# Sink attention in front of two expert layers: sink columns copied once, a row of steps one step later, a small scaling on another engine

## The chip, the cores and the metric

The kernel runs on one core of a Trainium2 chip. The time is that of one execution on the device, in microseconds (us). The core has five engines, each with a queue of its own that is worked off in order: TensorE (PE; PEld is its weight load), VectorE (DVE), ScalarE (ACT), GpSimd (POOL) and SyncE (SP), which only starts transfers here.

## The reference, cut to what matters

Three stages follow one another. The change touches only the first, and of it only batch 0 (and one preparation of the sink values in both batches).

```python
B, H, S, D = 2, 8, 768, 64; n_sink, window = 4, 128
scores = (q @ k.T) / sqrt(D)
keep = (key < n_sink) | ((query - key >= 0) & (query - key < window))
a = softmax(where(keep, scores, -1e9))
x = a @ v                                  # heads side by side: B, 768, 512
h = relu(x @ w_in)                         # 512 -> 1024; w_in, conv_w, w_out are float64
c = 3-tap convolution of h along the sequence, by conv_w
y = (h * sigmoid(c)) @ w_out               # 1024 -> 512
out = sum over 2 of 4 experts: w_e * causal_attention_e(y) @ wo_e
```

## The kernel before, in words

The sequence of 768 is cut into 6 tiles of 128 queries, and the 8 heads into 4 pairs. A step of the attention is one query tile `qt` and one head pair `pr`, so a batch has 24 steps, four to a tile. What belongs to one step is cut into stages (`S` scores, `T` transposes, `V` value products, `gather` and so on), and each stage has a lag in steps: at step t, the stage with lag L works on step t - L. `LAGS` holds the lags, and `ORD1` the order in which the stages of one step are written out; `run_phases` merges the stages of both batches and of the next layer by step and then by that order. So every engine's queue is a list fixed by hand. A stage with a third entry n works on n steps together, at the lag counted from the first of them. Batch 0's steps are followed by batch 1's, and from the sixth step of batch 1 on by those of the first expert layer.

In batch 0 the tiles `qt` 2 to 5 take an "overlaid" form (`a1_S_overlaid`, `a1_T_overlaid`), because with a window of 128 a query tile sees of the older key tile exactly the keys that it doesn't see of its own. Scores with the own key tile and with the older one go into two PSUM tiles (L515); VectorE overwrites one with the other where a mask says so (L518), takes the negative maximum of each row (L519) and scales it by 0.125 (L520); ScalarE takes the exponential with that as bias (L522), 132 columns wide for each head: 128 keys and 4 sink columns. The four sink columns come with the key tiles: an even key tile carries sinks 0 and 1 in front, an odd one must carry sinks 2 and 3 at its end. GpSimd copies them there (L511, 8 columns), once for each query tile 2 to 5, ahead of that tile's first scores.

The pairs `pr` 0 and 1, and 2 and 3, are transposed together (four transposes on TensorE, L571), copied from PSUM on ScalarE (L532), and split by GpSimd into the part of the own key tile and that of the older one (two selections, L575 and L577). The value products (L641) read these. The sink columns of the probabilities take another way: GpSimd gathers them pair by pair into a small tile `G` (L614) and, with the last pair, repeats that four times (L616); TensorE transposes it (`a1_sinkT`, L621), ScalarE copies it (L623), VectorE makes the low part of it (`a1_sinkL`, L628), and four products with the sink values `vsr` add it to the outputs (`a1_sinkV`, L649). The sums of the rows become reciprocals (`a1_r`), are transposed (`a1_rT`, L545), go to DRAM and come back spread over the partitions (L549, L556); `x_norm` multiplies the output by them (L560), `x_hi` and `x_lo` split the result into two parts (L532, L671), and `x_halo` copies edge columns.

`vsr` holds the sink values' high part in two groups of 32 partitions and the low part in the two others: ScalarE copies all (L295), then GpSimd subtracts in place in partitions 32 to 63 and 96 to 127, one instruction each (L299). Both sit in `tails`, a list from which each step takes one entry, in line with the pieces of a background job: the weights of the first expert layer, which arrive as float64, are decoded and split on VectorE and ScalarE during the attention (L343 to L353, L417, L538, L540).

The query, key and value tiles of the later part, the sums that come back and the outputs of most stages live in one pool of 18 SBUF buffers (tag `W`); a transfer into such a buffer waits for the last reader of what was there. PSUM has 8 banks under one tag (`B`), for scores, transposes and outputs alike.

Of the kernel before, what the change touches and what calls it, by code (L numbers as in the profile page):

```python
# [8 lines left out]
F32 = mybir.dt.float32  # L9
# [6 lines left out]
ALU = mybir.AluOpType  # L16
# [3 lines left out]
B, H, S, D = 2, 8, 768, 64  # L20
P = 128
NT = S // P
# [14 lines left out]
SCALE = 0.125  # L37
# [33 lines left out]
BG0 = 550  # L71
BG1 = 650
BG2 = 1200
LAGS = ((1, 2, 1, 5, 3, 4, 5, 5, 2, 7, 7, 9, 11), (1, 1, 2, 6, 3, 4, 5, 3, 2, 5, 6, 7, 7))
LAGM = (1, 2, 3)
A2_N = 2
EVT = 'aaadadada'
ORD1 = 'm.rest a0.more a1.T a0.gather m.more m.H a1.gather a1.rB m.gate a0.xl m.Y a1.S a1.V a1.sV a1.xl a1.r a0.S a1.halo a0.sL late a0.V a0.rB a0.sV a0.xm a1.more a1.sT a0.halo a0.rT a1.xm a1.misc a1.xh a0.sT a0.T a0.misc a1.sL a0.r a1.rT m.conv m.misc a0.xh'
ORD2 = 'q1 c0.V c0.T c0.S0 c1.V c1.T c1.S0 out c0.W c0.S1 qlo c0.norm c1.W in c1.S1 q0'
ENG_G = 'pp'  # L80
WHI = 'aadaddapdpaaddda'
# [7 lines left out]
class Kernel:  # L89
# [57 lines left out]
    def consts(self, pool):  # L147
        nc = self.nc
        self.words = pool.tile([P, 4], I32, name="words")
        self.ident = pool.tile([P, P], F32, name="ident")  # L150
        self.causal = pool.tile([P, 4 * P + 2], F32, name="causal")
        self.cw = pool.tile([P, 3 * NF], F32, name="cw")
        self.flag = pool.tile([P, 1], I32, name="flag")
        self.lims = pool.tile([P, 2], F32, name="lims")
        self.guard = pool.tile([P, 2 * NF + 1], F32, name="guard")
        self.ones = pool.tile([P, 1], F32, name="ones")
        self.nsink, self.window = self.lims[:, 0:1], self.lims[:, 1:2]
        self.m0 = pool.tile([P, P], F32, name="m0")
        self.m1 = pool.tile([P, 2 * P], F32, name="m1")
        self.mEO = [pool.tile([P, 2, KW], F32, name=f"m{i}x") for i in range(2)]  # L160
# [128 lines left out]

    def prep_vs(self, b, t):  # L290
        nc, vs = self.nc, t["vs"]

        def hi():
            t["vsr"] = self.pSm.tile([P, DM], F32R, tag="vsr", bufs=1, name=self.nm("vsr"))
            nc.scalar.copy(t["vsr"], vs)  # L295

        def lo(g):
            sl = slice(g, g + 32)
            nc.gpsimd.tensor_tensor(t["vsr"][sl], vs[sl], t["vsr"][sl].bitcast(F32), op=ALU.subtract)  # L299

        self.tails.append([hi, lambda: lo(32), lambda: lo(96)])


    def f64_ops(self, raw, n):
# [198 lines left out]
    def a1_S_overlaid(self, t, qt, pr, ps, Pt, nmx, sums):  # L503


        nc = self.nc
        w = KW + 2
        own, old = (x[:, : 2 * n].rearrange("p (j c) -> p j c", j=2) for x, n in zip(ps, (w, KW)))
        if pr == 0:
            odd = qt - 1 + qt % 2  # L510
            nc.gpsimd.tensor_copy(t["k"][:, odd, :, P:], t["k"][:, 0, :, 4:6])  # L511
        o = 2 * (qt % 2)
        for dst, kt in ((own[:, :, o : o + KW], qt), (old, qt - 1)):
            for j in range(2):
                nc.tensor.matmul(dst[:, j], t["q", qt][:, pr, j, :], t["k"][:, kt, pr, :], start=(j == 0), stop=(j == 1),  # L515
                                 skip_group_check=True)
        take = self.causal[:, 3 * P - o : 3 * P - o + KW].bitcast(I32)
        nc.vector.copy_predicated(own[:, :, 2 - o : 2 - o + KW], take[:, None, :].to_broadcast([P, 2, KW]), old)  # L518
        nc.vector.tensor_reduce(nmx, own, axis=AX.X, op=ALU.max, negate=True)  # L519
        nc.vector.tensor_scalar(nmx, nmx, SCALE, None, op0=ALU.mult)  # L520
        for j in range(2):
            nc.scalar.activation(Pt[:, j, :w], own[:, j], AF.Exp, bias=nmx[:, j : j + 1], scale=SCALE,  # L522
                                 accum_out=sums[:, j : j + 1])
# [39 lines left out]
    def a1_T_overlaid(self, b, qt, pr):  # L563


        if pr % 2 == 0:
            return
        nc = self.nc
        ps = self.psB().rearrange("p (a q) -> p a q", a=4)
        for i in range(4):  # L570
            nc.tensor.transpose(ps[:, i, :], self.a1P[(b, qt, pr - 1 + i // 2)][:, i % 2, 2 : 2 + P], self.ident)  # L571
        old, own = (self.Wt([P, 2, 2, P], s="PT") for _ in range(2))
        flat = [x.rearrange("p i j q -> p (i j) q") for x in (old, own)]
        self.copy(ENG_PT[b][(qt * NPAIR + pr) % len(ENG_PT[b])], flat[0], ps)
        nc.gpsimd.affine_select(out=flat[1], in_=flat[0], compare_op=ALU.is_ge, fill=0.0, base=0,  # L575
                                pattern=[[0, 4], [1, P]], channel_multiplier=-1)
        nc.gpsimd.affine_select(out=flat[0], in_=flat[0], compare_op=ALU.is_ge, fill=0.0, base=-1,  # L577
                                pattern=[[0, 4], [-1, P]], channel_multiplier=1)
        for i in range(2):
            del self.a1P[(b, qt, pr - 1 + i)]  # L580
            self.a1PT[(b, qt, pr - 1 + i)] = (old[:, i], own[:, i])

    def a1_T(self, b, qt, pr):
        if self.overlaid(b, qt):
            self.a1_T_overlaid(b, qt, pr)
            return
        nc = self.nc
        Pt = self.a1P.pop((b, qt, pr))
        if qt == 0:
            cols = [0]  # L590
        elif qt == 1:
            cols = [0, P]
        else:
            cols = [2, KW + 2]
        nb = len(cols)
        ps = self.psB().rearrange("p (j c q) -> p j c q", j=2, c=2)
        for j in range(2):
            for c, c0 in enumerate(cols):
                nc.tensor.transpose(ps[:, j, c, :], Pt[:, j, c0 : c0 + P], self.ident)  # L599
        PT = self.Wt([P, 2, 2, P], s="PT")  # L600
        self.copy(ENG_PT[b][(qt * NPAIR + pr) % len(ENG_PT[b])], PT[:, :, :nb], ps[:, :, :nb])
        self.a1PT[(b, qt, pr)] = [PT[:, :, c] for c in range(nb)]
# [79 lines left out]
    def attn_phase(self, b, start, lags, misc):  # L682
# [4 lines left out]
        def each(fn):  # L687
            return lambda i: fn(b, *steps[i])

        def last(fn, lo=0):  # L690
            def go(i):
                qt, pr = steps[i]
                if pr == NPAIR - 1 and qt >= lo:
                    fn(b, qt)

            return go

        st = {
            "r": (r, last(self.a1_r)), "rT": (rT, last(self.a1_rT)), "rB": (rB, last(self.a1_rB)),
            "xm": (xm, last(self.x_norm)), "S": (0, each(self.a1_S)), "T": (tr, each(self.a1_T)),  # L700
            "V": (pv, each(self.a1_V), 4 if b else 2), "gather": (gather, each(self.a1_gather)), "sT": (sT, last(self.a1_sinkT, 2)),
            "sL": (sL, last(self.a1_sinkL, 2)), "sV": (sV, last(self.a1_sinkV, 2)), "xh": (xh, last(self.x_hi)),
            "xl": (xl, last(self.x_lo)), "halo": (halo, last(self.x_halo)), "misc": (0, misc[0]), "more": (0, misc[1])}
# [2 lines left out]
    def attn_misc(self, b):  # L706
        def go0(i):
            if i == MASK_AT:
                self.more_masks()
            if i == NSTEP - 2:  # L710
                self.covered()
            if i == 6:
# [637 lines left out]
```

## Time and profile before

| | |
|---|---|
| median of 3 executions | 382.18 us (381.84 to 384.38) |
| the profiled execution's own time | 383.04 us |
| its span, first to last instruction | 381.2 us |
| PE busy | 359.4 us (94%) |
| DVE busy | 277.0 us (73%) |
| ACT busy | 257.5 us (68%) |
| POOL busy | 129.9 us (34%) |
| mean granted TensorE clock | 0.996 |

Batch 0's overlaid tiles run from about 18 to about 63 us of the span. In the rows further down, a time with an instruction is its start in us and its length; the square brackets behind it say how long the engine had been idle and whose work ended that.

### The profile page before, as it was taken

How to read it: one execution, taken by the hardware profiler on the slowest of the kernel's cores; microseconds unless marked ns; L12 is line 12 of the kernel's file. 1: busy time of each engine (PE TensorE's matmuls, PEld its weight loads, DVE VectorE, ACT ScalarE, POOL GpSimd, SP SyncE). 2: the span in 40 equal slices, each digit the busy share in tenths (PEclk: the TensorE clock that was granted, in tenths of full speed). 3: DMA queues.
4: the chain of work that ended last, by engine and by line, in shares of the span. 5: the costliest groups of instructions: out<-in, count | busy, mean ns of one | idle time of the engine just before them, and what ended most of it. 6: DMA issues, size and time to landing. Idle time of an engine off the chain costs nothing.

```text
span 381.2 us, 8949 instructions
## 1 busy us (share of the span) xinstructions
PE 359.4 (94%) x3198; PEld 333.8 (88%) x3198; DVE 277.0 (73%) x816; ACT 257.5 (68%) x770; POOL 129.9 (34%) x253
## 2 busy tenths in 40 slices
PE   8977787989999999999999999999999999999995
PEld 5666675879989999999999999999999899988984
DVE  5488988799989797878864776327778697669631
ACT  4865566776787676735655876438978698849841
POOL 7026344144442334365522222230015134506320
PEclk9999998999999999999999999999999999999999
DMA  8952466326242311010121001000000000101112
GB/s 176 346 147 88 143 212 197 106 93 217 89 140 85 110 57 40 19 30 3 44 61 43 21 3 57 0 2 1 2 3 0 3 29 28 58 3 55 41 47 90
DMA packets 21844, 27.51 MB, mean 72 GB/s; under 512 B 2112, under 2 KB 14496, under 8 KB 21792
## 3 DMA queue, kind: packets, MB, share of 16 engines
q1 hardware_dynamic: 20560, 26.21, 21.8%
q10 hardware_dynamic: 1232, 0.66, 0.8%
q8 instruction: 27, 0.44, 0.5%
q14 instruction: 25, 0.20, 0.2%
HBM read 23.66 MB, written 3.19 MB: 70 GB/s over the span
## 4 chain that ended last, share of the span: by engine, by line
PE 67%; DVE 12%; ACT 9%; POOL 6%; issue 3%; DMA 1%; SPq 0%; ACTq 0%; POOLq 0%; DVEq 0%
PE psB L852 15%; PE psB L808 13%; PE psB L1002 9%; PE psB L1126 5%; PE psB L930 5%; PE psB L1102 4%; PE psB L1150 3%; PE psB L641 3%; ACT P L497 2%; PE psB L480 2%; PE psB L1065 2%; PE psB L515 2%; PE psB L1064 2%; DVE P L494 2%; PE psB L599 2%
## 5 line engine op out<-in xcount | busy, mean ns | idle before, releaser
L852 PE MATMUL psB<-g,wouthf 128*128 128x256 f32 x384 | 70.4, 281 | 0.2
L852 PEld LDWEIGHTS psB<-g,wouthf 128*128 128x128 f32 x384 | 59.0, 188 | 0.6 <-POOL g L837 0.3
L1090 POOL TENSOR_SCALAR P<-P,r 128x256 f32<-128x256 f32 (+5 forms) x48 | 30.1, 640 | 82.7 <-DVE r L1088 42.6
L808 PE MATMUL psB<-xh,winhf 128*128 128x258 f32 x192 | 56.5, 294 | 0.0
L808 PE MATMUL psB<-xh,winlf 128*128 128x258 f32 x192 | 54.4, 283 | 0.0
L808 PE MATMUL psB<-xl,winhf 128*128 128x258 f32 x192 | 54.3, 283 | 0.0
L852 PE MATMUL psB<-g,woutlf 128*128 128x256 f32 x192 | 53.9, 281 | 0.0
L837 POOL TENSOR_TENSOR g<-ht,g 128x256 fp32r<-128x256 f32 x48 | 33.1, 689 | 52.5 <-ACT g L831 48.0
L824 ACT ACTIVATE ht<-ht 128x256 f32<-128x256 f32 x48 | 20.0, 418 | 28.3 <-DVE ht L822 28.3
L829 DVE SCALAR_TENSOR_TENSOR ht<-ht 128x256 f32<-128x256 f32 x48 | 24.2, 505 | 18.7 <-ACT ht L824 18.7
L497 ACT ACTIVATE P<-P,nm 128x260 f32<-128x260 f32 (+2 forms) x64 | 30.4, 477 | 10.6 <-DVE nm L494 10.5
L808 PEld LDWEIGHTS psB<-xh,winhf 128*128 128x128 f32 x192 | 36.4, 190 | 0.3
L808 PEld LDWEIGHTS psB<-xl,winhf 128*128 128x128 f32 x192 | 36.5, 190 | 0.0
L808 PEld LDWEIGHTS psB<-xh,winlf 128*128 128x128 f32 x192 | 36.3, 189 | 0.0
L852 PEld LDWEIGHTS psB<-g,woutlf 128*128 128x128 f32 x192 | 36.2, 188 | 0.0
L815 POOL TENSOR_SCALAR ht<-ht,cw 128x256 f32<-128x256 f32 x24 | 15.0, 624 | 58.4 <-ACT ht L811 50.8
L1075 ACT ACTIVATE P<-P,nm 128x256 f32<-128x256 f32 (+3 forms) x48 | 26.8, 561 | 4.6 <-DVE nm L1069 4.6
L822 DVE SCALAR_TENSOR_TENSOR ht<-ht,cw 128x256 f32<-128x256 f32 x48 | 28.3, 589 | 1.7
L1002 PE MATMUL psB<-yh,wqh 128*128 128x256 f32 x96 | 27.2, 283 | 0.0
L1002 PE MATMUL psB<-yl,wqh 128*128 128x256 f32 x96 | 27.0, 281 | 0.0
L1002 PE MATMUL psB<-yh,wql 128*128 128x256 f32 x96 | 27.0, 281 | 0.0
L1069 DVE CUSTOM_DVE_ANT_0 P<-psB,causal 128x256 f32<-128x256 f32 (+3 forms) x48 | 22.6, 486 | 5.9 <-PE psB L1065 5.7
(189 smaller groups left out, 1006.6 us busy)
## 6 DMA issues: line engine op xcount, KB each, us to landing
raw<-in_w_in_dram SPq DMA_DIRECT2D x8, 512.0 KB, 3.9
raw<-in_w_out_dram SPq DMA_DIRECT2D x8, 512.0 KB, 3.2
v<-in_v_dram SPq DMA_DIRECT2D x12, 256.0 KB, 5.4
R<-rD SPq DMA_DIRECT2D x24, 128.0 KB, 2.9
out_dram<-ot SPq DMA_DIRECT2D x11, 256.0 KB, 2.0
k<-in_k_dram SPq DMA_DIRECT2D x8, 260.0 KB, 3.7
raw<-in_wqkv_dram SPq DMA_DIRECT2D x8, 193.0 KB, 2.3
q<-in_q_dram SPq DMA_DIRECT2D x6, 256.0 KB, 3.4
```

What stands on the lines that cost most here:

```text
L497: nc.scalar.activation(Pt[:, j, :N], Pt[:, j, :N], AF.Exp, bias=nmx[:, j : j + 1], scale=-1.0, accum_out=sums[:, j : j + 1])
L808: nc.tensor.matmul(ps[:, :XW], w[:, f, kc, :], x[:, kc, :], start=(i == 0), stop=(i == len(ops) - 1))
L822: nc.vector.scalar_tensor_tensor(t1, h[:, 2 : 2 + CH], self.cw[:, 2 * NF + f : 2 * NF + f + 1], t1, op0=ALU.mult, op1=ALU.add)
L824: nc.scalar.activation(t1, t1, AF.Tanh)
L829: nc.vector.scalar_tensor_tensor(t1, t1, 1.0, h[:, 1 : 1 + CH], op0=ALU.add, op1=ALU.mult)
L837: eng.tensor_tensor(g[:, 1], t1, g[:, 0].bitcast(F32), op=ALU.subtract)
L852: nc.tensor.matmul(self.m1y[d // 2][:, d % 2, :], w[:, f, d, :], g[:, k], start=(first and i == 0 and d % 2 == 0), stop=(last and i == 2), ...
L930: nc.tensor.matmul(ps[:, :NVG], y[:, kc, ts_], w[:, kc, c0 : c0 + NVG], start=(i == 0), stop=(i == len(ops) - 1))
L1002: nc.tensor.matmul(ps, w[:, kc, c0 : c0 + P], y[:, kc, :], start=(i == 0), stop=(i == len(ops) - 1))
L1069: nc.vector.tensor_tensor_reduce(out=Pt[:, lo:hi], in0=ps[:, : hi - lo], in1=self.causal[:, 4 * P + lo - hi : 4 * P], scale=-1.0, scalar=B ...
L1075: nc.scalar.activation(Pt[:, lo:hi], src, AF.Exp, bias=nm[:, 0:1], scale=sg, accum_out=sums[:, j, i : i + 1])
L1090: nc.gpsimd.tensor_scalar(Ps[j][:, :N], Ps[j][:, :N], r[:, j : j + 1], 1.0, op0=ALU.mult, op1=ALU.mult)
```

## The change

It has six parts, all in the attention.

1. The sink columns are copied into the key tiles 1, 3 and 5 by three GpSimd instructions at step 2, behind the rest of the masks, in place of one at the first step of each of the tiles 2 to 5.
2. The transposes of the overlaid tiles become a stage of their own, `TT`, with lag 3 and both pairs of a group together, so one step later than before; `a0.TT` stands right behind `a0.T` in `ORD1`, which is otherwise as it was. What it issues (four transposes, ScalarE's copy, two selections) goes along.
3. In batch 0 the gathered sinks' transpose, low part and products, and the value products, have lags that are one greater (3, 4, 5, 5 become 4, 5, 6, 6); so have `x_norm`, `x_hi` and `x_lo` (7, 7, 9 become 8, 8, 10). The lags of the reciprocals, of their way through DRAM, of the gather and of `x_halo` stay.
4. The scaling of the maxima (128x2) goes from VectorE to ScalarE.
5. For the sink values ScalarE multiplies by a column of zeros and ones in place of copying, and GpSimd does one subtraction over all 128 partitions in place of two over 32 each. The list `tails` gets one entry less for that, so the pieces behind it move up by one step.
6. Four GpSimd memsets of 32x1 fill that column once.

```diff
-LAGS = ((1, 2, 1, 5, 3, 4, 5, 5, 2, 7, 7, 9, 11), (1, 1, 2, 6, 3, 4, 5, 3, 2, 5, 6, 7, 7))
+LAGS = ((1, 2, 1, 6, 4, 5, 6, 5, 2, 8, 8, 10, 11), (1, 1, 2, 6, 3, 4, 5, 3, 2, 5, 6, 7, 7))
...
     def prep_vs(self, b, t):
         nc, vs = self.nc, t["vs"]
+        if b == 0:
+            for g in range(0, P, 32):
+                nc.gpsimd.memset(self.below[g : g + 32], float(g // 32 % 2))
...
-            nc.scalar.copy(t["vsr"], vs)
-
-        def lo(g):
-            sl = slice(g, g + 32)
-            nc.gpsimd.tensor_tensor(t["vsr"][sl], vs[sl], t["vsr"][sl].bitcast(F32), op=ALU.subtract)
-
-        self.tails.append([hi, lambda: lo(32), lambda: lo(96)])
+            nc.scalar.mul(t["vsr"], vs, self.below)
+
+        def lo():
+            nc.gpsimd.tensor_tensor(t["vsr"], vs, t["vsr"].bitcast(F32), op=ALU.subtract)
+
+        self.tails.append([hi, lo])
...
-        if pr == 0:
-            odd = qt - 1 + qt % 2
-            nc.gpsimd.tensor_copy(t["k"][:, odd, :, P:], t["k"][:, 0, :, 4:6])
...
-        nc.vector.tensor_scalar(nmx, nmx, SCALE, None, op0=ALU.mult)
+        nc.scalar.mul(nmx, nmx, SCALE)
...
     def a1_T_overlaid(self, b, qt, pr):
-        if pr % 2 == 0:
+        if pr % 2 == 0 or not self.overlaid(b, qt):
             return
...
     def a1_T(self, b, qt, pr):
         if self.overlaid(b, qt):
-            self.a1_T_overlaid(b, qt, pr)
             return
...
-            "xm": (xm, last(self.x_norm)), "S": (0, each(self.a1_S)), "T": (tr, each(self.a1_T)),
+            "xm": (xm, last(self.x_norm)), "S": (0, each(self.a1_S)), "T": (tr, each(self.a1_T)), "TT": (3, each(self.a1_T_overlaid), 2),
...
             if i == MASK_AT:
                 self.more_masks()
+                k = self.qkv[0]["k"]
+                for tt in range(1, NT, 2):
+                    self.nc.gpsimd.tensor_copy(k[:, tt, :, P:], k[:, 0, :, 4:6])
```

## Rows read from the trace of the kernel before

**Rows 1.** The chain that ended last, 31.42 to 39.39: start, length (us), what.
```profile
31.42 0.63 POOL PT L575
...
33.05 1.26 POOL vsr L299
...
34.62 0.27 POOL G L616
...
38.50 0.14 POOL k L511
38.67 0.71 PE psB L515 x4
```

**Rows 2.** Waits of 20 to 70 us, PE: us in total, times, longest.
```profile
PE psB L621 <- POOL G L616: 6.6, 4, 2.7
PE psB L515 <- POOL k L511: 4.1, 3, 2.3
PE psB L649 <- DVE SPT L628: 1.0, 1, 1.0
```

**Rows 3.** Busy time by stretch: length, then PE, PEld, DVE, ACT, POOL; PE clock.
```profile
20.00:40.00 20.00, 14.56 (x147) 12.50 (x146) 16.45 (x40) 12.95 (x48) 9.30 (x20) 1.00 0.41 120
40.00:60.00 20.00, 15.47 (x159) 13.46 (x157) 18.36 (x51) 12.21 (x48) 8.26 (x23) 1.00 0.55 171
60.00:70.00 10.00, 8.28 (x75) 6.25 (x72) 7.23 (x29) 7.03 (x30) 2.73 (x9) 0.83 0.56 178
...
50.00:60.00 10.00, 8.22 (x85) 7.05 (x83) 9.30 (x29) 6.51 (x25) 4.16 (x11) 1.00 0.52 172
```

**Rows 4.** The same in single microseconds, around the fall of PE's clock.
```profile
62.00:63.00 1.00, 0.27 (x3) 0.08 (x1) 0.94 (x5) 1.00 (x7) 0.93 (x2) 1.00 0.96 373
63.00:64.00 1.00, 0.00 (x1) 0.01 (x1) 1.00 (x3) 0.70 (x4) 0.94 (x7) 0.93 0.14 47
...
66.00:67.00 1.00, 1.00 (x14) 1.00 (x12) 0.94 (x6) 0.88 (x4) 0.00 (x0) 0.50 0.56 201
```

**Rows 5.** DVE's L520 alone, by stretch and over all: min/median/max ns.
```profile
20.00:40.00 20.00, 3.06 (x8) 1.00 0.41 120
40.00:60.00 20.00, 2.17 (x8) 1.00 0.55 171
...
L520 DVE TENSOR_SCALAR nm<-nm x16: 169/273/1011, 20.0 to 57.9; 128x2 f32<-128x2 f32 x16
```

**Rows 6.** ACT by line, whole span: idle time of L813; smallest form.
```profile
L813 ACT ACTIVATE ht<-ht,cw 128x256 f32<-128x256 f32 x24 | 12.3, 512 | 0.8
...
L1234 ACT ACTIVATE e<-zeros 128x1 f32<-128x1 bf16 x1 | 0.2, 202 | 0.0
```

**Rows 7.** Timeline of the start: key tiles, first scores, GpSimd.
```profile
5.67 1.47 PE L492 MATMUL psB<-k,q 128*128 128x128 f32 x8 [0.53 <-DMA k<-in_k_dram]
8.70 0.19 POOL L222 TENSOR_SCALAR m1x<-snk 128x2 f32<-128x2 f32 x1
9.62 1.04 PE L492 MATMUL psB<-k,q 128*128 128x256 f32 x4
10.78 0.43 SPq L265 DMA_DIRECT2D k<-in_k_dram  x1
16.51 0.19 POOL L511 COPY k<-k 128x8 f32<-128x8 f32 x1 [7.62 <-PE psB L492]
```

**Rows 8.** POOL by line and form: the subtractions.
```profile
L874 POOL TENSOR_TENSOR yl<-y,yh 128x512 fp32r<-128x512 f32 x6 | 8.4, 1418 | 0.5 <-ACT yh L878 0.5
...
L299 POOL TENSOR_TENSOR vsr<-vs,vsr 32x512 fp32r<-32x512 f32 x4 | 5.5, 1386 | 1.8 <-issue 1.5
```

**Rows 9.** DMA issues on the page: KB each, median us to landing.
```profile
k<-in_k_dram SPq DMA_DIRECT2D x8, 260.0 KB, 3.7
```

**Rows 10.** Waits in SP's queue, to 130 us: us in total, times, longest.
```profile
SPq L556 <- PE psB L641: 5.2, 3, 2.8
```

More of the change, by code (lines that the diff above doesn't have):

```diff
@@ L77 @@
 EVT = 'aaadadada'
-ORD1 = 'm.rest a0.more a1.T a0.gather m.more m.H a1.gather a1.rB m.gate a0.xl m.Y a1.S a1.V a1.sV a1.xl a1.r a0.S a1.halo a0.sL late a0.V a0.rB a0.sV a0.xm a1.more a1.sT a0.halo a0.rT a1.xm a1.misc a1.xh a0.sT a0.T a0.misc a1.sL a0.r a1.rT m.conv m.misc a0.xh'
+ORD1 = 'm.rest a0.more a1.T a0.gather m.more m.H a1.gather a1.rB m.gate a0.xl m.Y a1.S a1.V a1.sV a1.xl a1.r a0.S a1.halo a0.sL late a0.V a0.rB a0.sV a0.xm a1.more a1.sT a0.halo a0.rT a1.xm a1.misc a1.xh a0.sT a0.T a0.TT a0.misc a1.sL a0.r a1.rT m.conv m.misc a0.xh'
 ORD2 = 'q1 c0.V c0.T c0.S0 c1.V c1.T c1.S0 out c0.W c0.S1 qlo c0.norm c1.W in c1.S1 q0'
@@ L156, in consts @@
         self.ones = pool.tile([P, 1], F32, name="ones")
+        self.below = pool.tile([P, 1], F32, name="below")
         self.nsink, self.window = self.lims[:, 0:1], self.lims[:, 1:2]
```

## The prediction

> **What bounds the kernel now.** Whole-span shares (PE 94%) say little; I read the stretch that the change touches. First the waits, by engine: between 20 and 70 us TensorE waits 11.7 us in eight places, and all but one of them end with a GpSimd instruction [rows 2]. The reader should see that GpSimd, idle for more than half of that stretch [rows 3], is nevertheless what TensorE waits for: not its work but its queue is late. The chain of waits shows how [rows 1]. The selections L575 and L577 at 31.42 wait for the transposes' copy on ScalarE; the subtraction L299 stands behind them, and only then come the last gather and L616, at 34.62. The transpose of the gathered sinks, L621, stands in TensorE's queue ahead of the next scores and waits 2.7 us for it. At 38.50 the same queue delivers an 8-column copy of sink keys, and the next tile's scores start on it. Then I read busy time by stretch [rows 3], to see what stands behind the waits. VectorE is full for 0.82 of 20 to 40, 0.92 of 40 to 60 and 0.93 of 50 to 60; ScalarE has about a third free. So TensorE's waits from 40 on lie largely beside VectorE's work, and freeing TensorE alone would gain little there. Last the clock: TensorE, idle for its last wait from 62.3 to 64.0, is granted 0.5 of full speed (1.2 in place of 2.4 GHz) from about 63.9 on [rows 4]; a mean of 0.83 over ten us [rows 3] makes that 0.17 x 10 / 0.5 = 3.4 us.
>
> **The change, part by part.** I first ask of each wait where it goes, then add up what each engine has left.
>
> *Copies of the sink columns.* Four 0.19 us copies go from the tiles' first steps, three come at step 2. The 4.1 us of waits on them [rows 2] go. At step 2 GpSimd has just ended the masks, at 8.9, and has nothing to do until 16.5 [rows 7]. The copy into key tile 1 would run from 8.9 to about 9.1; the scores of query tile 1, which start at 9.62 and in this trace are tied to that copy by a wait (it waited for their last one) [rows 7], would find it done. The copies into tiles 3 and 5 stand behind it and wait for their tiles to land, the last at about 10.78 + 3.7 = 14.5 [rows 7, 9]; queued behind them are only the first gathers, which can't come before the first exponentials, after 20 us [rows 5]. Cost on the path: nothing; if the cover fails, see the second rival.
>
> *Transposes, gathered sinks and value products.* Per query tile the stage order on TensorE becomes: scores 0, products of the tile two back; scores 1, sink products, the sums' transpose, transposes; scores 2, products of the tile before; scores 3, gathered sinks, transposes. The gather of the last pair keeps its lag, so L621 comes two steps behind it in place of one, and the selections of the same tile's last pairs now stand behind the gather in GpSimd's queue, not ahead. A step is some 2.5 us (15 of them between the first and the last of the scalings, at 20.0 and 57.9 [rows 5]), about as long as the longest wait, 2.7 us; the 6.6 us go. The selections still have three steps until the products read them, as before. The 1.0 us that the sink products wait for their low part is one case, at the border to batch 1; the low part moves together with them, so I count it neither way in the sum. No work is added: the moved copies on ScalarE and selections on GpSimd only change their places, and VectorE's `x_norm`, `x_lo` and low parts come once per tile as before. No DMA is moved, but probabilities and the returned sums stay in the 18 buffers up to a step longer, so a transfer in SP's queue could be held; such waits now cost the loads of the sums 5.2 us in three places [rows 10], with nobody waiting for them in [rows 2]. I price that between 0 and one step once, 2.5 us, and take 0, because the reader of those sums, `x_norm`, also moves a step back.
>
> *Maxima.* VectorE loses 16 instructions, 3.06 us in 20 to 40 and 2.17 us in 40 to 60; undisturbed one takes 0.169, the mean is 0.33 and the longest 1.01 [rows 5], which ran beside GpSimd's L299 of 33.05 [rows 1]. ScalarE gets 16, each between 0 (wholly in the waits for VectorE) and 0.2 us, the smallest activation of the trace; that ScalarE waits for its own result is cheap here, since the dependent L813 shows 0.8 us of idle time in 24 cases [rows 6]. I take 0.2, so 1.6 us in each stretch. Behind the waiting scaling on ScalarE stand the same exponentials that waited for VectorE before.
> The Trainium skill (ScalarE: Activation LUTs, Rules for kernel authors) says to use VectorE, not ScalarE, for a multiplication. Undisturbed, the rule holds here by the rows too: 16 x (0.20 - 0.17) = 0.5 us would be lost if every scaling were on the path; by the mean of rows 5 the same count gives back 16 x (0.33 - 0.20) = 2.1 us.
>
> *Sink values.* On GpSimd one 128x512 subtraction, 1.42 us, replaces two of 32x512, 1.39 each [rows 8], so 1.35 us less per batch, and the memsets are of its smallest kind. In batch 0 nobody waits any more. In batch 1 VectorE meets one of them less; the nearest row for such a meeting is the longest L520, 1.01 in place of 0.17 [rows 5], so it is worth 0 to 0.8, and I take 0.4. The background pieces move a step forward and stay as many: 0.
>
> *The sum.* Once nobody waits for GpSimd, a stretch lasts as long as its fullest engine, divided by how full it can be. From 20 to 40: TensorE 14.6 (VectorE 16.45 - 3.06 = 13.4, ScalarE 12.95 + 1.6 = 14.6). From 40 to 60: VectorE 18.36 - 2.17 = 16.2 (TensorE 15.5, ScalarE 13.8). From 60 to 70: VectorE 7.2, with TensorE at 8.28 less half of the 3.4 us at half clock, 6.6 [rows 3 to 5]. How full? VectorE reached 0.93 and TensorE 0.82 in 50 to 60 [rows 3]; after the change three engines are close to each other, which leaves more gaps than one full one, so I take the middle, 0.875: 16.7 + 18.5 + 8.2 = 43.4 in place of 50, a gain of 6.6. With 0.93 it is 15.7 + 17.4 + 7.7 = 40.8, a gain of 9.2; with 0.82 it is 17.8 + 19.8 + 8.8 = 46.4, a gain of 3.6. With 0.4 for batch 1 the gain is 7.0 (3.6 to 10.0). What follows after 70 is the same queues, begun earlier; nothing there hangs on the clock on the wall, as loads are issued by step. The profiled execution took 383.04 (span 381.2 and 1.8 around it), so 376.0; it was 0.9 above the median, so the median becomes 375.2, between 372.2 and 378.6.
>
> **The rivals.** *VectorE is already the bound.* From 40 us on it is 0.92 full, its results free the PSUM banks that the next scores need, and ScalarE's longer queue frees them no sooner. Then TensorE's waits after 40 only change their names, and what remains is the key-copy waits of 20 to 40, where VectorE had 3.5 us free: 2.3 us for the longest and 0.4 for another, a gain of 2.7, so 379.5. Against it: VectorE's own list gets 2.2 us shorter there.
>
> *The start stalls.* If the scores of query tile 1 wait for GpSimd's third copy and not its first, they start at 14.5 + 0.2 = 14.7 in place of 9.62, 5.1 us late, and a wait longer than that of [rows 4] would be followed by a like stretch at half clock, 1.7 more: 6.8. It decides from the moment that the awaited copy lies behind the load issued at 10.78. Against a gain of 7.0 that gives 382.0, against 3.6 it gives 385.4, so on the whole slower than before. Against it: tile 0's scores ran at 5.67, before the later key tiles were even asked for [rows 7], so accesses are told apart by key tile, and the first copy is the one that overlaps.
>
> *All waits vanish.* TensorE keeps its 38.3 us [rows 3] less 1.7 of slow clock without gaps, VectorE never holds it: a gain of 11.7 + 1.7 = 13.4 at most, 368.8; anything from 10 on belongs here.
>
> **How the numbers follow.** Forecast 0.68, VectorE the bound 0.16, start stalls 0.07, all waits vanish 0.09. The range takes in the forecast's bounds, the first rival and a part of the last: 371 to 381. One per cent, 3.8 us, is about what a measurement of this kernel can tell from no change. Faster by more: 0.68 and 0.09, less 0.02 for the forecast's upper edge, 0.75. Within 1%: the first rival, that edge and a small part of the stall, 0.20. Slower by more, 0.05: the rest of the stall, with a clock that stays low longer.
>
> **What would show it.** Right: in 20 to 65 us no TensorE wait on L616's and L511's successors; the scaling on ScalarE near 0.2 us; the first scores of tile 1 near 9.6; the last scores' exponentials of batch 0, behind the scaling that is now at 57.9, at about 53; clock 1.0 through the 3.4 us that are now slow; PE and VectorE both near 0.87 full in the attention. Wrong: TensorE waits of similar length on ScalarE's exponentials or copies (banks), a GpSimd wait ahead of query tile 1, a late `x_norm` behind its transfer, or the gain visible at 53 us and gone by 110, where VectorE, less rested, would hold the expert layer.

## The result and the profile after

The changed kernel takes 378.64 us (378.52 to 379.84, 4 executions), the kernel before beside it 382.87 (381.84 to 384.38, 4): a ratio of 0.9894 [0.9851, 0.9936], so 4.2 us faster where 7.0 were forecast. Two more measurements of the same kernel, made beside the experiments below, gave 0.9907 [0.9877, 0.9936] and 0.9893 [0.9862, 0.9925]. The profiled execution took 378.69 us, with a span of 377.0.

Where the time came from is read with milestones rather than with whole-span shares, because everything behind the changed stretch is the same list of instructions. The first one is the start of batch 1's scores. A line's own view gives it: line, engine, count, min/median/max ns, first to last start. First before, then after (some lines of the file stand up to 3 further down or up there).

```profile
L480 PE MATMUL psB<-k,q x176: 272/272/580, 57.1 to 156.0; 64*128 64x130 f32 x128, 64*128 64x128 f32 x48
```
```profile
L483 PE MATMUL psB<-k,q x176: 272/272/376, 51.5 to 151.5; 64*128 64x130 f32 x128, 64*128 64x128 f32 x48
```

So 5.6 us are gained by then. The same view of the first expert layer's products (L808, L852 before; L810, L854 after) gives the next two milestones: 70.4 and 84.8 before, 64.8 and 79.9 after. The stretch up to 70.4 (64.8) took 13.3 us in both kernels, the next 14.4 before and 15.1 after, and the rest 296.4 and 297.1. The gain has thus been made by the end of the overlaid tiles (0.3 of it ahead of them: they start at 17.4 in place of 17.7), and 1.4 of it is lost again behind them.

TensorE's waits between 20 and 70 us, in the columns of [rows 2]:

```profile
PE psB L545 <- DVE su L528: 2.2, 3, 0.8
PE psB L483 <- DVE psB L518: 1.5, 1, 1.5
PE psB L545 <- ACT nm L520: 1.1, 1, 1.1
PE psB L515 <- DVE psB L518: 0.7, 1, 0.7
PE psB L648 <- DVE SPT L627: 0.4, 1, 0.4
PE psB L515 <- ACT P L522: 0.2, 1, 0.2
```

Every wait for GpSimd is gone, the 6.6 us on the gathered sinks and the 4.1 on the key copies [rows 2]. Of 11.7 us, 6.1 are left, and all of them end with VectorE or ScalarE. Busy time by stretch, in the columns of [rows 3]; the first four lines answer to the four there, the fifth to those of [rows 4]:

```profile
20.00:40.00 20.00, 17.51 (x173) 15.39 (x173) 18.01 (x39) 15.31 (x62) 9.73 (x23) 1.00 0.45 144
40.00:60.00 20.00, 16.27 (x166) 13.56 (x163) 18.43 (x50) 14.66 (x61) 10.43 (x24) 1.00 0.59 186
60.00:70.00 10.00, 9.94 (x102) 8.39 (x102) 9.06 (x30) 7.71 (x31) 2.78 (x9) 1.00 0.51 162
50.00:60.00 10.00, 7.49 (x72) 5.84 (x73) 8.73 (x29) 7.56 (x31) 5.34 (x13) 1.00 0.49 160
...
63.00:64.00 1.00, 1.00 (x11) 0.71 (x12) 0.90 (x4) 1.00 (x5) 0.00 (x0) 1.00 0.88 261
```

The granted clock is 1.00 in all of these stretches; the one at 0.5 of [rows 4] is gone. VectorE, which was to become lighter, is 0.90 full in 20 to 40 and 0.92 in 40 to 60. The scaling, now on ScalarE, and the start (timeline: start, length, engine, instruction):

```profile
L520 ACT ACTIVATE nm<-nm x16: 186/204/226, 19.6 to 54.0; 128x2 f32<-128x2 f32 x16
```
```profile
9.05 0.45 POOL L711 COPY k<-k 128x8 f32<-128x8 f32 x3
9.50 0.82 PE L495 MATMUL psB<-k,q 128*128 128x256 f32 x3
```

The copies run at once, all three by 9.50, and the scores of tile 1 start where they started before [rows 7].

To see where VectorE's gain went, the same stretches by milestone, first before, then after:

```profile
17.70:57.10 39.40, 30.39 (x303) 26.67 (x303) 32.94 (x83) 24.99 (x94) 16.24 (x40) 1.00 0.51 154
57.10:70.40 13.30, 10.58 (x94) 8.14 (x92) 10.13 (x38) 8.52 (x34) 4.05 (x13) 0.87 0.51 161
```
```profile
17.40:51.50 34.10, 30.39 (x295) 26.74 (x295) 29.62 (x65) 25.27 (x103) 15.42 (x35) 1.00 0.53 163
51.50:64.80 13.30, 10.73 (x107) 8.12 (x107) 12.34 (x39) 10.55 (x43) 6.76 (x18) 1.00 0.63 200
```

Over the two VectorE has 17 instructions fewer (16 scalings, and one `x_lo` that now comes later) and yet only 1.1 us less to do (43.07 to 41.96), where the scalings alone were 5.2 [rows 5]. Its lines show why (count, busy us, mean ns, idle before). Before:

```profile
L518 DVE COPY_PREDICATED psB<-causal,psB 128x260 f32<-128x260 int32 x16 | 6.8, 424 | 5.7 <-PE psB L515 5.7
L350 DVE SCALAR_TENSOR_TENSOR f64u<-raw,f64u 128x512 int32<-128x512 int32 x5 | 3.5, 695 | 0.0
L671 DVE TENSOR_TENSOR xl<-R,xh 128x512 fp32r<-128x512 f32 x5 | 3.4, 689 | 0.1
L527 DVE TENSOR_SCALAR su<-su 128x8 f32<-128x8 f32 x6 | 1.0, 164 | 0.0
```

After, the same four (L350 is now L353, L671 is L670):

```profile
L518 DVE COPY_PREDICATED psB<-causal,psB 128x260 f32<-128x260 int32 x16 | 6.8, 426 | 2.2 <-PE psB L515 2.2
L353 DVE SCALAR_TENSOR_TENSOR f64u<-raw,f64u 128x512 int32<-128x512 int32 x5 | 5.2, 1033 | 0.0
L670 DVE TENSOR_TENSOR xl<-R,xh 128x512 fp32r<-128x512 f32 x4 | 4.2, 1059 | 0.0
L527 DVE TENSOR_SCALAR su<-su 128x8 f32<-128x8 f32 x6 | 2.7, 458 | 0.0
```

Three lines with the same work became slower by 1.7 us (5 x 0.34), 1.5 (4 x 0.37) and 1.8 (6 x 0.29), 4.9 together; those with an operand in PSUM, as L518, did not. The timeline shows beside what they ran, GpSimd's two selections:

```profile
27.18 0.87 POOL L575 TENSOR_SCALAR_AFFINE_SELECT PT<-PT 128x512 f32<-128x512 f32 x1 [4.12 <-ACT PT L532]
27.46 0.61 DVE L527 TENSOR_SCALAR su<-su 128x8 f32<-128x8 f32 x1
...
28.11 0.64 POOL L577 TENSOR_SCALAR_AFFINE_SELECT PT<-PT 128x512 f32<-128x512 f32 x1
28.27 1.03 DVE L670 TENSOR_TENSOR xl<-R,xh 128x512 fp32r<-128x512 f32 x1
```

An instruction of 0.16 us takes 0.61 and ends with the selection at 28.05; one of 0.69 takes 1.03. The selections suffer too: L575 has a mean of 710 ns before and 880 after, L577 704 and 805. The scalings that met GpSimd before, up to 1.01 us [rows 5], have gone from VectorE. Whether these three lines meet it now because the scalings left, or because the selections moved, is parted by u23 and u4 below.

### The profile page after: what moved, and what is told of

Its sections match the earlier page's. It is cut to its first block, busy times and chain, and to the rows that moved or that the text cites. A ratio compares the mean times of both kernels' runs of the same rounds, so it can differ in the third digit from the quotient of the medians.

```text
span 377.0 us, 8947 instructions
## 1 busy us (share of the span) xinstructions
PE 359.7 (95%) x3198; PEld 333.8 (89%) x3198; DVE 275.9 (73%) x800; ACT 259.9 (69%) x786; POOL 132.0 (35%) x254
## 4 chain that ended last, share of the span: by engine, by line
PE 65%; DVE 10%; ACT 6%; issue 2%; POOL 1%; DMA 1%; ACTq 0%; DVEq 0%
PE psB L854 15%; PE psB L810 14%; PE psB L1004 9%; PE psB L1128 5%; PE psB L932 5%; PE psB L1104 4%; PE psB L1152 3%; PE psB L640 2%; PE psB L1067 2%; PE psB L1066 2%; PE psB L483 2%; PE psB L598 1%; ACT P L1077 1%; ACT P L500 1%; DVE P L497 1%
## 5 line engine op out<-in xcount | busy, mean ns | idle before, releaser
L854 PE MATMUL psB<-g,wouthf 128*128 128x256 f32 x384 | 70.4, 281 | 0.3 <-POOL g L839 0.2
L854 PEld LDWEIGHTS psB<-g,wouthf 128*128 128x128 f32 x384 | 58.9, 188 | 0.7 <-POOL g L839 0.5
L810 PE MATMUL psB<-xh,winhf 128*128 128x258 f32 x192 | 56.6, 295 | 0.0
L810 PE MATMUL psB<-xl,winhf 128*128 128x258 f32 x192 | 54.3, 283 | 0.0
L810 PE MATMUL psB<-xh,winlf 128*128 128x258 f32 x192 | 54.2, 282 | 0.0
L854 PE MATMUL psB<-g,woutlf 128*128 128x256 f32 x192 | 53.8, 280 | 0.0
L810 PEld LDWEIGHTS psB<-xh,winhf 128*128 128x128 f32 x192 | 36.4, 189 | 0.3 <-ACT ht L813 0.2
L810 PEld LDWEIGHTS psB<-xl,winhf 128*128 128x128 f32 x192 | 36.5, 190 | 0.0
L810 PEld LDWEIGHTS psB<-xh,winlf 128*128 128x128 f32 x192 | 36.3, 189 | 0.0
L854 PEld LDWEIGHTS psB<-g,woutlf 128*128 128x128 f32 x192 | 36.2, 188 | 0.0
L817 POOL TENSOR_SCALAR ht<-ht,cw 128x256 f32<-128x256 f32 x24 | 15.5, 648 | 56.9 <-ACT ht L813 51.4
```

Source lines behind the costliest of these rows:

```text
L810: nc.tensor.matmul(ps[:, :XW], w[:, f, kc, :], x[:, kc, :], start=(i == 0), stop=(i == len(ops) - 1))
L854: nc.tensor.matmul(self.m1y[d // 2][:, d % 2, :], w[:, f, d, :], g[:, k], start=(first and i == 0 and d % 2 == 0), stop=(last and i == 2), ...
```

## The experiments

The theory at this point: waits on GpSimd's queue gave the gain, and VectorE's collisions with the selections took back what the forecast had counted for 60 to 70. Rivals: one part alone (copies, later steps or scaling) gave it all; VectorE's load, or a wait elsewhere, explains the loss. Each kernel differs from the changed one by the edit shown, unless it says otherwise. The table gives the median, the ratio to the kernel before as measured alongside, and for the profiled execution the starts of batch 1's scores, of the expert layer's products and of its output products, and the span.

| kernel | us | ratio [95%] | scores | products | outputs | span |
|---|---|---|---|---|---|---|
| before | 382.87 | | 57.1 | 70.4 | 84.8 | 381.2 |
| changed | 378.64 | 0.9894 [0.9851, 0.9936] | 51.5 | 64.8 | 79.9 | 377.0 |
| u1, copies per tile | 392.63 | 1.0250 [1.0215, 1.0284] | 64.9 | 78.3 | 93.0 | 390.1 |
| u23, old lags | 380.22 | 0.9935 [0.9903, 0.9967] | 53.4 | 65.7 | 80.3 | 376.9 |
| u4, scaling on VectorE | 380.42 | 0.9929 [0.9901, 0.9957] | 53.2 | 66.3 | 81.3 | 378.4 |
| n5, no selections | 374.52 | 0.9770 [0.9740, 0.9801] | 49.6 | 61.2 | 75.8 | 372.7 |
| changed, again | 379.71 | 0.9907 [0.9877, 0.9936] | 51.4 | 66.0 | 80.8 | 377.6 |
| b1, before + copies once | 380.78 | 0.9937 [0.9914, 0.9961] | 55.2 | 68.1 | 82.3 | 379.2 |
| whi_a | 380.52 | 0.9926 [0.9900, 0.9952] | 52.3 | 66.2 | 81.7 | 378.8 |
| xl9 | 389.12 | 1.0139 [1.0107, 1.0172] | 59.2 | 76.3 | 91.1 | 387.4 |
| changed, third time | 379.15 | 0.9893 [0.9862, 0.9925] | 51.4 | 64.8 | 79.8 | 376.5 |
| u5, two subtractions | 378.78 | 0.9886 [0.9856, 0.9916] | 50.8 | 64.2 | 79.5 | 376.4 |
| rt3 | 378.58 | 0.9876 [0.9845, 0.9906] | 52.0 | 64.6 | 79.6 | 376.9 |
| rt3_r | 378.10 | 0.9866 [0.9836, 0.9897] | 51.6 | 64.1 | 79.1 | 376.3 |

**The copies undone (u1).**

```diff
-                k = self.qkv[0]["k"]
-                for tt in range(1, NT, 2):
-                    self.nc.gpsimd.tensor_copy(k[:, tt, :, P:], k[:, 0, :, 4:6])
...
+        if pr == 0:
+            odd = qt - 1 + qt % 2
+            nc.gpsimd.tensor_copy(t["k"][:, odd, :, P:], t["k"][:, 0, :, 4:6])
```

> The changed kernel with the sink columns copied again at the first step of each of the tiles 2 to 5; all else as changed. Queue theory (the gain came because GpSimd's late queue no longer stands in front of TensorE): each copy now stands behind the selections of the tile before, TensorE waits 1 to 2 us on it at three tiles, batch 1's first scores move from 51.5 to 54 to 56 us, and the time is 2 to 4 us above the changed kernel's. Rival (VectorE is full anyway, so the copies cost nothing): TensorE waits on the copy, but batch 1's first scores stay within 0.7 us of 51.5 and the time within 0.7 us of the changed kernel's.

It lost some 14 us, far more than either theory allowed: the change without its first part is slower than before. The wait and its place in the queue (scores are L518, copies L514 here):

```profile
PE psB L518 <- POOL k L514: 13.4, 3, 4.6
```
```profile
26.91 0.64 POOL L578 TENSOR_SCALAR_AFFINE_SELECT PT<-PT 128x512 f32<-128x512 f32 x1 [4.11 <-ACT PT L535]
27.62 0.63 POOL L580 TENSOR_SCALAR_AFFINE_SELECT PT<-PT 128x512 f32<-128x512 f32 x1
...
28.40 0.21 POOL L514 COPY k<-k 128x8 f32<-128x8 f32 x1
...
28.66 2.06 PE L518 MATMUL psB<-k,q 128*128 128x130 f32 x8 [4.56 <-POOL k L514]
```

With the transposes a step later, the selections stand ahead of the next tile's copy, so its scores wait for the end of the tile before: TensorE drains three times. The clock falls behind the wait, as in [rows 4]: from 30 to 32 us it is 0.50, and 20 to 40 and 40 to 60 have means of 0.91 and 0.83. Part 2 depends on part 1.

**The later steps undone (u23)**, all lags and that of `TT` as before, copies and scaling as changed.

```diff
-LAGS = ((1, 2, 1, 6, 4, 5, 6, 5, 2, 8, 8, 10, 11), ...
+LAGS = ((1, 2, 1, 5, 3, 4, 5, 5, 2, 7, 7, 9, 11), ...
...
-    ... "TT": (3, each(self.a1_T_overlaid), 2),
+    ... "TT": (2, each(self.a1_T_overlaid), 2),
```

> The changed kernel with the lags and the place of the transposes as before; copies once, scaling on ScalarE and the single subtraction stay. Queue theory: the waits for the gathered sinks come back (some 5 of the 6.6 us of before), batch 1's first scores come at 54 to 56 us and the time is 2 to 3.5 us above the changed kernel's. Rival (the copies and the shorter VectorE list made the gain, the later steps none): first scores of batch 1 within 1 us of 51.5, time within 0.7 us of the changed kernel's.

```profile
PE psB L620 <- POOL G L615: 7.0, 4, 3.4
```
```profile
L670 DVE TENSOR_TENSOR xl<-R,xh 128x512 fp32r<-128x512 f32 x5 | 3.5, 699 | 0.1
L353 DVE SCALAR_TENSOR_TENSOR f64u<-raw,f64u 128x512 int32<-128x512 int32 x5 | 3.5, 697 | 0.0
L527 DVE TENSOR_SCALAR su<-su 128x8 f32<-128x8 f32 x6 | 1.0, 165 | 0.0
...
17.40:53.40 36.00, 30.39 (x305) 26.54 (x303) 29.43 (x69) 27.63 (x111) 15.86 (x41) 1.00 0.54 168
53.40:65.70 12.30, 10.52 (x94) 8.09 (x92) 9.19 (x36) 8.72 (x35) 4.04 (x12) 0.86 0.53 169
...
35.14 0.63 POOL L575 TENSOR_SCALAR_AFFINE_SELECT PT<-PT 128x512 f32<-128x512 f32 x1 [1.44 <-ACT PT L532]
35.32 0.43 DVE L518 COPY_PREDICATED psB<-causal,psB 128x260 f32<-128x260 int32 x1 [1.87 <-PE psB L515]
35.79 0.43 DVE L519 TENSOR_REDUCE nm<-psB 128x2 f32<-128x264 f32 x1
35.84 0.63 POOL L577 TENSOR_SCALAR_AFFINE_SELECT PT<-PT 128x512 f32<-128x512 f32 x1
```

All of the wait on the gathered sinks is back, 7.0 us of it, but batch 1's scores start only 1.9 us later and the median is 0.5 to 1.6 above the three of the changed kernel: between the two forecasts, with intervals that overlap. VectorE's rows show why so long a wait is worth so little. With the transposes at their old step the three slow lines have their old lengths, although the scalings are gone. VectorE's work up to the expert layer is 38.62 us (29.43 + 9.19), 4.4 less than in the kernel before, with just the 16 scalings fewer. So the later steps rid TensorE of 7.0 us of waits and give VectorE 3.3 us more to do (41.96). The last four lines show where the selections stand at the old step: mostly beside instructions that read PSUM, L518 and L519 above all, and these keep their 0.43 us.

The profiled execution is the shortest of the eight, 378.65 us at a mean granted clock of 0.995, as short as the changed kernel's (378.69 at 0.996); the longest took 382.27, at 0.978. So these two profiles show no gain in time from the later steps, and what the median shows goes at least in part with the clock.

**The scaling undone (u4).**

```diff
-        nc.scalar.mul(nmx, nmx, SCALE)
+        nc.vector.tensor_scalar(nmx, nmx, SCALE, None, op0=ALU.mult)
```

> The changed kernel with the scaling of the maxima back on VectorE. Theory (after the change VectorE bounds the attention of batch 0, and what its list lost in scalings it got back in collisions with GpSimd's selections): VectorE gets 16 x 0.17 = 2.7 us of work back, so batch 1's first scores come 1.5 to 3 us later than 51.5 and the time is 1.5 to 2.5 us above the changed kernel's. Rival (TensorE and ScalarE share the bound, the scaling is hidden on either engine): within 0.5 us. Second rival (the scalings were the main gain): 4 us or more.

```profile
L520 DVE TENSOR_SCALAR nm<-nm 128x2 f32<-128x2 f32 x16 | 2.9, 180 | 0.6
...
17.50:53.20 35.70, 30.39 (x295) 26.73 (x295) 31.59 (x80) 22.94 (x91) 15.72 (x36) 1.00 0.52 156
```

Batch 1's scores start 1.7 us later, the median is 0.7 to 1.8 higher, with intervals that overlap. The first line is the main thing: in the new order the same 16 scalings cost VectorE 2.9 us, not 5.2, since they no longer meet GpSimd (mean 180 ns in place of 327). In the tiles VectorE has 2.0 us more to do (31.59 against 29.62) and is 0.88 full (0.87 in the changed kernel), which speaks for VectorE's list setting the pace there. L353 and L527 are as slow as in the changed kernel (1032 and 453 ns), though the scalings are back on VectorE: it is the later step that puts these two beside the selections, and not that the scalings left.

**The copies alone (b1)**: the kernel before, with the copies made once at step 2.

> The kernel before with the sink columns copied once at step 2 and nothing else changed. Queue theory, amended by the first runs (the copies' waits are most of what stood on the path, the waits for the gathered sinks lay largely beside VectorE's work): the copies' 4.1 us of waits vanish, those for the gathered sinks stay at 6 to 8 us, batch 1's first scores come at 53.5 to 55, and the time is 1.5 to 3 us below the kernel before, so some half of the whole change's gain. Rival (only the later steps free the path, the waits change their names): within 1 us of the kernel before.

The gain is 2.6 us (383.37 to 380.78; batch 1's scores, at 55.2, come a little behind the forecast) of the 3.7 that the changed kernel had beside it. The waits on the gathered sinks are untouched (6.6 us in 4). So the copies give more than half of the gain; by u23 and u4, later steps and scaling add little one at a time (2.9 and 2.7 us under before) and some 1 to 2 us together. Each of these differences is uncertain by 1 us or more.

With b1 there are four kernels for two questions. VectorE's work in us, from the start of the tiles to that of the expert layer's products (with the later step one `x_lo`, 0.69 us, falls behind the end):

| | scaling on VectorE | scaling on ScalarE |
|---|---|---|
| transposes at the old step | 42.6 (b1) | 38.6 (u23) |
| one step later | 43.8 (u4) | 42.0 (changed) |

Moving the scaling takes 4.0 us from VectorE at the old step (the sink values' preparation changes along with it) and 1.8 at the later one.

**No selections (n5).**

```diff
-        nc.gpsimd.affine_select(out=flat[1], in_=flat[0], ...)
-        nc.gpsimd.affine_select(out=flat[0], in_=flat[0], ...)
...
-            self.a1PT[(b, qt, pr - 1 + i)] = (old[:, i], own[:, i])
+            self.a1PT[(b, qt, pr - 1 + i)] = (old[:, i], old[:, i])
...
```

> The changed kernel without the two selections L575 and L577 (the products of the overlaid tiles then use both key tiles' probabilities unselected, so this part of the computation is left out). Collision theory (VectorE instructions that run beside a GpSimd selection are held up; that took the 4 us that VectorE's list should have lost): the three long groups return to their old means (L353 from 0.98 to 0.69 us, the low part L670 from 1.06 to 0.69, L527 from 0.50 to 0.16), batch 1's first scores come at 49 to 50.5 us, the first expert layer's first products at 61 to 63 in place of 64.8, and the time is 2 to 4 us below the changed kernel's. Rival (the collisions lie in VectorE's idle time, or TensorE bounds): means fall the same way, the time stays within 0.7 us of the changed kernel's.

It took 374.52 us, 4.1 to 5.2 below the three measurements of the changed kernel, more than was expected. Its lines on VectorE, and its stretch from 49.6 (batch 1's scores) to 61.2:

```profile
L353 DVE SCALAR_TENSOR_TENSOR f64u<-raw,f64u 128x512 int32<-128x512 int32 x5 | 3.4, 685 | 0.0
L527 DVE TENSOR_SCALAR su<-su 128x8 f32<-128x8 f32 x6 | 1.0, 166 | 0.0
...
49.60:61.20 11.60, 10.49 (x108) 7.99 (x108) 10.48 (x40) 10.33 (x43) 1.33 (x8) 1.00 0.70 229
```

Two of the slowed lines have their old lengths, 685 for 1033 and 166 for 458 ns; of `x_lo`, three take 0.64 us, and one takes 1.37 beside GpSimd's subtraction L302. The tiles take 32.2 us in place of 34.1, and the next stretch 11.6 in place of 13.3, with VectorE's work there at 10.48 in place of 12.34. That is 1.7 us, the gain that the forecast had for this stretch. The run also shortens GpSimd's queue and holds one buffer of the 18 less for each pair of steps; as TensorE waited nowhere for GpSimd from 20 to 70 us in the changed kernel, I put the gain to the collisions, but the run doesn't part the three.

**Less work on VectorE (whi_a)**: three of the 16 weight pieces' first scaling (L540, 128x512) go to ScalarE.

```diff
-WHI = 'aadaddapdpaaddda'
+WHI = 'aaaaaaapdpaaddda'
```

> The changed kernel with three scalings of weight pieces (high parts, 128x512, 0.42 us each on VectorE) moved to ScalarE, where one takes 0.62 us. VectorE-bound theory: batch 1's first scores 0.2 to 0.6 us earlier than 51.5, the expert layer's first products 0.8 to 1.5 us earlier than 64.8, time 0.5 to 1.5 us below the changed kernel's. Rival (ScalarE is as full as VectorE): time the same within 0.4 us or up to 1 us more.

No gain; with 380.52 it stands 0.8 above the changed kernel measured alongside (379.71). The three pieces, 0.42 us each, ran on VectorE at 40.0, 58.4 and 66.8 us, one in the tiles and one in each stretch behind them, and up to 66 us VectorE's wait for the pieces that ScalarE makes rose from 1.9 to 3.0 us:

```profile
DVE winlf L420 <- ACT winhf L538: 3.0, 4, 1.1
```

So taking work from VectorE doesn't help if VectorE then waits for it; the run doesn't tell more than that.

**Another step for the low part (xl9)**, to move `x_lo` away from the selections.

```diff
-LAGS = ((1, 2, 1, 6, 4, 5, 6, 5, 2, 8, 8, 10, 11), ...
+LAGS = ((1, 2, 1, 6, 4, 5, 6, 5, 2, 8, 8, 9, 11), ...
```

> The changed kernel with the low part of the outputs (x_lo) one step earlier, at lag 9 as it was. Collision theory: the five subtractions, which take 0.88 to 1.06 us beside GpSimd's selections now, fall back to about 0.69 if their new place has no selection; that is 1.5 us less for VectorE and 0.5 to 1.2 us less in time. Rival (the selection then holds up what stands in their place): the means move to another instruction and the time stays within 0.4 us.

Both theories missed. `x_lo` was freed of GpSimd (median 691 ns), but it stands at the head of VectorE's step, and its source `x_hi` at the end of ScalarE's:

```profile
DVE xl L670 <- ACT xh L532: 7.2, 4, 2.1
...
PE psB L648 <- DVE SPT L627: 5.7, 3, 2.4
PE psB L545 <- DVE su L528: 4.6, 3, 4.0
```

VectorE's 7.2 us of waiting reach TensorE, and the time goes up by 9.4 (389.12 against 379.71). The clock falls too: its means are 0.83, 0.91 and 0.83 in 20 to 40, 40 to 60 and 60 to 80, where the changed kernel has 1.00, so part of the 9.4 is TensorE at half speed. The step of lag was worth more here than the collision that it avoided.

**The two subtractions back (u5)**, without the memsets.

```diff
-            nc.scalar.mul(t["vsr"], vs, self.below)
+            nc.scalar.copy(t["vsr"], vs)
...
-        self.tails.append([hi, lo])
+        self.tails.append([hi, lambda: lo(32), lambda: lo(96)])
```

> The changed kernel with the sink values' preparation as before (copy on ScalarE, two subtractions over 32 partitions each, one entry more in the list of pieces). Theory of the prediction (one meeting of VectorE with a long GpSimd subtraction fewer per batch): the time is 0 to 0.8 us above the changed kernel's. Rival (the pieces of the background job that moved up by a step cost what the stretch from 64.8 to 79.8 lost, 15.0 us in place of 14.4): that stretch takes 14.3 to 14.6 us again and the time is 0.3 to 0.8 us below the changed kernel's.

378.78 against 379.15 for the changed kernel alongside: no difference. The stretch in which the 0.7 us were lost took 15.3 us, so neither the subtraction nor the shifted list of background pieces is their cause. VectorE's collision there did come back (13.56 us of work from 64.2 to 79.5, with one instruction more in it, against 12.66 from 64.8 to 79.9), without any effect on the end.

**The sums' transpose later (rt3), and the reciprocals ahead of background pieces (rt3_r).** TensorE's longest remaining waits are those of L545 for the sums, so their transpose gets a step more; rt3_r also writes `a0.r` ahead of `a0.misc`.

```diff
-LAGS = ((1, 2, 1, 6, 4, 5, 6, 5, 2, 8, 8, 10, 11), ...
+LAGS = ((1, 2, 1, 6, 4, 5, 6, 5, 3, 8, 8, 10, 11), ...
...
-ORD1 = '... a0.T a0.TT a0.misc a1.sL a0.r a1.rT ...'
+ORD1 = '... a0.T a0.TT a0.r a0.misc a1.sL a1.rT ...'
```

> The changed kernel with the transpose of the row sums' reciprocals one step later (lag 3 in place of 2). Theory (after the change TensorE's main wait, 3.3 us before 70 us, is this transpose, which stands in its queue ahead of the transposes and the next scores and waits for reciprocals that VectorE reaches late): those waits go to under 1 us, batch 1's first scores come 0.5 to 2 us before 51.5, and the time is 0.5 to 1.5 us below the changed kernel's. Rival (VectorE and ScalarE set the pace, the wait lies beside their work): the wait changes its name, time within 0.4 us.

> As the one before, and the reciprocals' two instructions stand ahead of the background piece of their step on VectorE. Theory (the reciprocals, L527, are held up by a selection because the background piece pushes them beside it): L527's mean falls from 0.46 to 0.2 to 0.3 us, and the time is 0 to 0.7 us below that of the run with the later transpose alone. Rival (the selection then holds up the next instruction): within 0.3 us of it.

The waits at L545 are gone, and in rt3 others have taken their place: 3.3 us at L515, for VectorE's L518 and ScalarE's L522, where there were 0.9. That is the rival, a wait that only changes its name: batch 1's scores come no earlier (52.0 against 51.4), and the 0.6 us between the medians lie within the noise. In rt3_r the mean of L527 falls to 0.27 us, as its theory had it; the 0.5 us against rt3 lie within the noise too. rt3_r is the fastest kernel of the study at 378.10, 0.9866 [0.9836, 0.9897], clearly ahead of before; against the changed kernel it is 1.05 us better alongside (379.15), which the intervals don't part.

## Why the prediction was right, and which of its steps failed

The sign and the range held: 378.6 lies between 371 and 381, 3.4 above the point; 0.7 of that is the kernel before, 382.87 here and 382.18 there. Step by step:

- **Copies cost nothing: right in its effect, wrong in one detail.** They were to wait for their tiles' landing until 14.5; all three had run by 9.50. The rival of the stalled start is out.
- **Gathered sinks, 6.6 us of waits go: right.** They went, and the products that follow wait nowhere long. That they are not worth 6.6 us was in the sum already, which divided each engine's work by its fullness; u23 shows it, 7.0 us of waits for 0.5 to 1.6. That so little is left of them comes of the step that failed, below.
- **20 to 60, 4.8 us: right in size, partly by luck**, 5.6 at batch 1's scores. TensorE is 0.89 and VectorE 0.87 full there (30.39 and 29.62 of 34.1), with 0.875 forecast. But VectorE's work fell by 3.3 us there (32.94 to 29.62) and not by 5.2, and the later steps push work past this milestone: between it and the expert layer TensorE has 107 products in place of 94.
- **"No work is added: the moved copies on ScalarE and selections on GpSimd only change their places": the step that failed**, and with it "VectorE loses 16 instructions, 3.06 us in 20 to 40 and 2.17 us in 40 to 60". VectorE lost 1.1 us in all. The price of the scalings held for the order in which it was read: with the transposes at their old step (u23) VectorE loses 4.4 of the 5.2. The later step takes 3.3 us of that back. It moves the selections, which stood mostly beside instructions that they don't slow (L518, L519), to beside L353, L527 and `x_lo`, which became 4.9 us longer. In that order the scalings would have cost only 2.9 us (u4), so less was left to gain by taking them away. The step looked at where the selections stood in GpSimd's queue and not at what would then run beside them on VectorE.
- **60 to 70, 1.8 us: not there**, and this follows from the same step. The stretch up to the expert layer took 13.3 us before and after, though its slow clock [rows 4] and the wait ahead of it are gone. TensorE got free and VectorE, 0.76 full before (10.13 of 13.3), is 0.93 full now (12.34); of the 2.2 us more, about 1.7 are the lengthening of the three lines, the rest is work that comes later. u23 takes 12.3 us for the stretch with 9.19 us of VectorE's work, although its clock falls there (0.86), and n5 without the selections gives 1.7 us back. As the milestone in between cuts the work differently, the two stretches together are the surer number: 5.6 us gained by the expert layer's start, where 6.6 were forecast. The changed kernel's second profile shows it from the other side. There the clock did fall, from 54 to 60 us:

```profile
52.00:54.00 2.00, 0.62 (x4) 0.51 (x6) 1.97 (x4) 0.38 (x3) 1.42 (x5) 0.93 0.85 264
54.00:60.00 6.00, 6.00 (x39) 4.89 (x39) 4.90 (x17) 5.21 (x21) 2.89 (x7) 0.50 0.56 178
```

Half speed for 6 us is 3 us of TensorE's work, yet the expert layer starts 1.2 later and the span is 0.6 longer: with VectorE as full as this, I read, most of a slow TensorE is hidden.
- **Scaling on ScalarE at 0.2 each: right** (median 204 ns), and worth 0.7 to 1.8 us by the medians (u4), with intervals that overlap. The Trainium skill's advice to leave a multiplication to VectorE (ScalarE: Activation LUTs, Rules for kernel authors) is not borne out here even at VectorE's undisturbed 0.18, since VectorE has less room than ScalarE (29.62 and 25.27 us busy of the 34.1).
- **Batch 1, 0.4 us, and "what follows after 70 is the same queues, begun earlier": not so.** VectorE did meet one subtraction less, and its work in the stretch from 64.8 is 0.4 us less (13.07 to 12.66), but the stretch took 0.7 longer and the rest 0.7 (0.3 in the third profile). TensorE's lines there have the same counts (one transpose apart) and mean lengths within 7 ns in both kernels, and its granted clock is 1.00, yet its transposes (L599, now L598) and batch 1's scores fill 0.9 us more. u5 took the subtraction out as a cause. By the table the stretch took 14.2 to 14.6 us in the three kernels with the old lags (before, b1, u23) and 14.6 to 15.5 in all others, so it seems to come with the later steps; why, stays open.

The gain was forecast at 7.0 and is 4.2. The 2.8 between them: 1.8 for the missing stretch, 0.4 for batch 1 and 1.4 lost behind 64.8, less 0.8 that the tiles gave above their forecast. The first rival, VectorE as the bound, was half right: from 40 us on VectorE did hold the kernel, but, as far as n5 shows it, through collisions that the later steps brought along and not through its old work.

## What to carry to other kernels

A stage that moves takes its collisions along: before moving one, ask which instructions of the other engine will run beside it at the new place. The same 16 scalings, taken from VectorE, were worth 4.0 us of its work with the selections at their old step and 1.8 with them a step later. In a queue worked off in order, a stage may be moved only together with everything that other engines await behind it: the same later transposes are part of a gain of 3.7 to 4.6 us with the copies done early and of a loss of 9.5 us with them left in place. A wait of several microseconds on one engine is worth only what the next-fullest engine leaves free beside it, less what ending the wait adds to that engine.

## What the runs showed of the hardware that was not expected

Beside GpSimd's selections over 128x512, VectorE instructions with both ends in SBUF took 0.46 us on average in place of 0.16 (L527) and 1.03 in place of 0.69 (L353), and the selections are held too; those that read PSUM (L518 424 and 426 ns, L560 688 and 681) kept their length to 1%. Not every such meeting costs VectorE time: an L356 over 128x512 that started at 36.66, 0.04 us ahead of a selection, took its usual 0.69 us, and the selection took 1.15 in place of 0.64. The Trainium skill (SBUF — State Buffer, Who interferes with whom) says that a VectorE instruction with two SBUF inputs, or in a two-port mode, shares a port pair with GpSimd, and that whoever issues second is held completely. These rows agree on who meets whom and on the order. The L527 at 27.46 ends with the selection, as complete holding would have it; the `x_lo` at 28.27 was held 0.34 us where 0.48 of the selection were left, a little less than that.

The clock answered differently to nearly the same idle time. In all three profiles of the changed kernel TensorE waits 1.5 us for L518 ahead of batch 1's scores, at about 52; in the first and the third the clock stays at 1.00, in the second it is 0.50 from 54 to 60. And the kernel before spread over 3.2 to 3.6 us beside the experiments (11 to 18 executions each), the changed one over 1.5 and 1.6 (6 each). The mean granted clock of each execution goes with the time in part: u23's eight run from 378.65 us at 0.995 to 382.27 at 0.978, in nearly the same order, while for the kernel before the order is looser (beside u23, 381.15 us at 0.996 and 384.68 at 0.991). What else adds to the spread was not looked for.
